# Delta rule, router and two expert layers on one core: the fourth key product in eight wide matmuls, the triangle solved by output rows, single first and last solve steps, and later key loads

## The chip, the cores and the metric

One Trainium2 chip; the program runs on one of its cores. The metric is device microseconds of one execution of the whole program.

## What is computed

Three layers follow one another: a delta rule over 4 x 8 heads of 768 tokens with 48 values each, a router with 8 experts of 384 x 1024, and a dense layer of 384 x 2048 with a squared relu. The change touches the first:

```
k_n = k / (norm(k) + 1e-6)
state = 0                                   # 48 x 48 for each of the 32 heads
for t in range(768):
    y[t]  = q[t] @ state
    v_old = state.T @ k_n[t]
    state = state + beta[t] * outer(k_n[t], v[t] - v_old)
x = y, as 3072 rows of 384
x = gate * (relu(x @ w1[expert]) @ w2[expert])    # expert = argmax of x_n @ e_n / tau
out = relu(x @ w_in) ** 2 @ w_out
```

## The kernel before, in words

The 768 tokens are cut into 24 chunks of 32, four chunks make a group (6 groups). Within a chunk the rule becomes a lower triangular system of 32 x 32 for each head, so that a group has 128 lanes (4 chunks x 32 heads and batches), one to a partition.

- **Products of keys** (`gram`, L138 to L185, called through `grams` at the start and in the chunk loop later): for each chunk 64 small TensorE matmuls of 64 x 32 against 32 columns (keys only, `n1 = 1`) or 64 columns (keys and queries). ScalarE evicts them (L169) into `GPs` (key by key, one tile per group) and `Pm` (key by query). For groups 0 and 1 VectorE turns `GPs` into lanes (L204, four 32 x 32 block transposes); for later groups that goes through DRAM (`gscr`, L171 and L174). `Pm` goes through DRAM for all groups (`pscr`, L179, then `PL2`, L183). These DMAs are on the queue of SP, which issues in order and waits for each one's input.
- **The solve** (`lanes`, L191 to L283): for one group a list of VectorE instructions. The norms come from the squares of the first keys (group 0) or from the diagonal of the products, by three Newton steps (`newton`, L78). `factors` (L223) makes `gam`; `scale` multiplies the products with its negative (L212). Then 31 steps in which `mul(j)` (L264) multiplies column j of the products with what is solved, and `acc(j)` (L272) adds it to the triangle `T`; four transposes (`end`, L277) put the result into `TTt`. Between the last steps stand `vh` (L254, values times norms) and `masked` (L189).
- **Order.** The instructions are issued in the order in which the Python calls are made. At the start (L728 to L783) the loads are issued, then `grams(0, 1, 0, 4, 0)`, 26 instructions of group 0's list, each followed by one of `route_q` (the router's own Newton steps on 8 rows), more products, and from the point at which 15 units of group 0's list are left, one instruction of group 1 before each of group 0.
- **The chunk loop** (L786 on): in each chunk VectorE makes `Ub` (L319) from `CH`, TensorE multiplies it with `TTt` (L338), ScalarE and VectorE evict that as `Wb` (L351, L319), TensorE updates the state (L357), ScalarE evicts it (`Sb`, L367), and the next chunk's `CH` is the state times its keys (L308). `fill` puts instructions of the groups ahead in between, by a budget that is worked out while the program is written.
- **Loads.** `load_kq` (L120) fetches keys and queries of a chunk, for chunks 0 to 14 on SP, from 15 on by GpSimd. Chunks 12 to 14 are fetched at L768, 15 to 17 at L856, in the code behind the first chunk, but nothing holds GpSimd until then. `padding` (L535) fills a piece of the router's table with one row by GpSimd; it is called in the chunk loop for chunks 0 to 8.
- **After the loop** the experts (each product in three fp32r matmuls of high and low parts) and the last layer run; TensorE is full there.

Of the kernel before, what the change touches and what calls it, by code (L numbers as in the profile page):

```python
# [8 lines left out]
F32 = mybir.dt.float32  # L9
# [13 lines left out]
def kernel(  # L23
# [54 lines left out]
    def newton(ops, y, ss, t, half):  # L78
        ops.append(lambda: V.tensor_scalar(y.bitcast(I32), ss.bitcast(I32), 1, None, ALU.logical_shift_right))
        ops.append(lambda: V.tensor_tensor(y.bitcast(I32), half, y.bitcast(I32), ALU.subtract))  # L80
        for _ in range(3):
            ops.append(lambda: V.tensor_tensor(t, y, ss, ALU.mult))
            ops.append(lambda: V.scalar_tensor_tensor(t, t, -0.5, y, ALU.mult, ALU.mult))
            ops.append(lambda: V.scalar_tensor_tensor(y, t, 1.5, y, ALU.add, ALU.mult))
        ops.append(lambda: V.tensor_tensor(y, y, ss, ALU.mult))
        ops.append(lambda: V.tensor_scalar(y, y, 1e-6, None, ALU.add))

# [53 lines left out]
    def gram(s, n0=0, n1=2, banks=GP2):  # L141
# [33 lines left out]
        if i == 3 and n1 == 2:  # L175
# [9 lines left out]
            )  # L185

    def masked(g, b):
        a = PL2[g][:, b].rearrange("p s c j -> p (s c) j")
        V.tensor_tensor(a, a, mask.unsqueeze(1).broadcast_to([128, 8, C]), ALU.mult)  # L189

    def lanes(g):  # L191
# [18 lines left out]
        def scaled(c0, c1):  # L210
            a = AL[:, c0:c1, c0 + 1 :]
            V.tensor_tensor(a, a, t1[:, c0 + 1 :].unsqueeze(1).broadcast_to(list(a.shape)), ALU.mult)  # L212

# [9 lines left out]
        def factors():  # L223
            add(lambda: V.reciprocal(r, nl))
            add(lambda: V.tensor_tensor(r, r, r, ALU.mult))
            add(lambda: V.tensor_tensor(gam, r, betaL[:, g], ALU.mult))
            add(lambda: V.tensor_scalar(t1, gam, -1.0, None, ALU.mult))

        nw = []
        if g == 0:  # L230
            add(lambda: V.tensor_reduce(ss, kn[0], AX.X, ALU.add))
            newton(nw, nn, ss, t1, magic)
# [28 lines left out]
        def mul(j):  # L261
            n, m = j + 1, 31 - j
            tv[0] = wp.tile([128, 256], F32, name=f"tmp{g % 2}")[:, : m * n].rearrange("p (c i) -> p c i", c=n)
            V.tensor_tensor(  # L264
                tv[0],
                AL[:, j, j + 1 :].unsqueeze(1).broadcast_to([128, n, m]),
                T[:, :n, j : j + 1].broadcast_to([128, n, m]),
                ALU.mult,
            )

        def acc(j):
            V.tensor_tensor(T[:, : j + 1, j + 1 :], T[:, : j + 1, j + 1 :], tv[0], ALU.add)  # L272

        def end(i):
            if i == 0:
                TTl[g] = wp.tile([128, C, C], F32, name="TTt", bufs=2)
            V.transpose(  # L277
                TTl[g].rearrange("p u i -> p i u")[:, i : i + 8], T.rearrange("p c i -> p i c")[:, i : i + 8]
            )

        for j in range(31):
            for f in (mul, acc):
                add(lambda f=f, j=j: f(j), (31 - j) * (j + 1))  # L283
# [367 lines left out]
    def attention():  # L651
# [91 lines left out]
        route_q.extend(router_consts())  # L743
        A.activation(kn[0], kn[0], AF.Square)
        consts()
# [11 lines left out]

        grams(0, 1, 0, 4, 0)
        st0 = Stream(0, 0)
        streams.append(st0)  # L760
        for _ in range(26):
            st0.pop()
            if len(route_q) > 1:
                route_q.popleft()()
        warm(2)
        grams(0, 2, 4, 8, 0)
        load_k2(0)
        grams(1, 2, 0, 4, 1)  # L768
        for s in range(12, 15):
            load_kq(s)  # L770
        load_v(1)
        load_k2(1)
        grams(0, 2, 8, 12, 1)
        st1 = Stream(1, 0)
# [12 lines left out]
        for s in range(NS):  # L787
# [61 lines left out]
            if last and i == 0:  # L849
                R[1]()  # L850
                queue(R[2])
                scats += R[3]
            if s <= E:
                padding(s)
            if s == 0:
                for n in range(15, 18):  # L856
                    load_kq(n)
            if i == 3 and g + 2 < NG:
# [597 lines left out]
```

## Time and profile before

| | |
|---|---|
| median of 3 runs | 931.98 us (930.43 to 934.85) |
| the profiled execution | 926.72 us |
| its span, from the first to the last instruction | 925.0 us |
| TensorE busy | 868.9 us (94%) |
| VectorE busy | 592.3 us (64%) |
| ScalarE busy | 443.2 us (48%) |
| GpSimd busy | 104.0 us (11%) |
| mean granted TensorE clock | 0.966 |

The shares are means over parts with different limits, so they are read by stretches. A line of the trace has the start and the duration in microseconds, the engine, the line of the program, the operation with the tile it writes, an arrow and the tiles it reads, the shape, and how many instructions it stands for; in brackets stands how long the engine was idle before it, and what ended that. PE is TensorE's matmul, PEld its weight load, DVE VectorE, ACT ScalarE, POOL GpSimd, SPq and POOLq the queues that issue DMAs.

### The profile page before, as it was taken

To read this page: it belongs to the slowest core of one execution; us is meant where nothing else is said; L and a number is where in the kernel's file an instruction comes from. 1 tells how busy PE (TensorE), PEld (TensorE's weight loads), DVE (VectorE), ACT (ScalarE), POOL (GpSimd) and SP (SyncE) were. 2 spreads that over 40 slices of the span, in tenths; PEclk is the share of its full clock that TensorE was granted. 3 is DMA by queue.
4 is the path that set the end of the run, shared out by engine and by line. 5 is a ranking of instruction groups with operands and counts; after the bars stand their busy time and mean duration, and the time that the engine had idled before them with its cause. 6 is when DMAs were issued, how large, how long until landed. Compare 5 with 4: busy or idle time off the path is not lost.

```text
span 925.0 us, 22005 instructions
## 1 busy us (share of the span) xinstructions
PE 868.9 (94%) x8859; PEld 792.9 (86%) x8859; DVE 592.3 (64%) x1478; ACT 443.2 (48%) x1074; POOL 104.0 (11%) x138
## 2 busy tenths in 40 slices
PE   3668999999989899999999999999999999999998
PEld 2446677667678799899988999999999999999998
DVE  6999799999767788879776762517061524425150
ACT  2246778778834565465645642415051423324140
POOL 3012103212211122122222100000000000000000
PEclk7587899999999999999999999999999999999999
DMA  8786876332247778557673532010010101020000
GB/s 328 247 270 204 237 196 189 117 142 70 75 147 183 266 267 285 181 198 274 223 243 102 175 83 43 1 45 7 28 25 18 35 18 35 9 43 10 18 1 26
DMA packets 103678, 117.12 MB, mean 127 GB/s; under 512 B 60339, under 2 KB 82202, under 8 KB 103568
## 3 DMA queue, kind: packets, MB, share of 16 engines
q1 hardware_dynamic: 95344, 89.25, 31.5%
q0 software_dynamic: 8064, 26.35, 7.9%
q8 instruction: 75, 1.23, 0.6%
q14 instruction: 35, 0.29, 0.1%
q10 hardware_dynamic: 160, 0.01, 0.0%
HBM read 83.47 MB, written 32.89 MB: 126 GB/s over the span
## 4 chain that ended last, share of the span: by engine, by line
PE 65%; DMA 1%; ACT 0%; another core or an unknown queue 0%; DVE 0%; SPq 0%; issue 0%; ACTq 0%
PE gp L1158 8%; PE gp L1159 8%; PE gp L1160 8%; PE xp L1158 5%; PE xp L1160 5%; PE xp L1159 5%; PE sp L1159 4%; PE sp L1158 4%; PE sp L1160 4%; PE yp L1159 3%; PE yp L1160 3%; PE yp L1158 3%; PE gp L1284 1%; PE ch L981 1%; PE ch L1158 1%; PE ch L1159 1%
## 5 line engine op out<-in xcount | busy, mean ns | idle before, releaser
L1364 DVE TENSOR_TENSOR t4k<-t2k 128x384 f32<-128x384 f32 x128 | 71.3, 557 | 203.8 <-ACT t2k L1363 201.9
L1158 PE MATMUL xp<-wb,hh 128*128 128x384 f32 x184 | 62.5, 340 | 0.0
L1159 PE MATMUL xp<-wb,hh 128*128 128x384 f32 x184 | 62.1, 338 | 0.0
L1160 PE MATMUL xp<-wb,hl 128*128 128x384 f32 x184 | 62.1, 338 | 0.0
L272 DVE TENSOR_TENSOR TL<-TL,tmp 128x135 f32<-128x135 f32 (+15 forms) x186 | 60.8, 337 | 1.8
L264 DVE TENSOR_TENSOR tmp<-AL,TL 128x135 f32<-128x135 f32 (+15 forms) x186 | 60.5, 336 | 1.6
L1307 POOL DMA_INDIRECT x<-y,rows x32 | 37.8, 1182 | 195.6 <-ACT y L1304 123.0
L1158 PE MATMUL sp<-xh,W 128*128 128x384 f32 (+1 forms) x156 | 53.1, 340 | 0.8 <-ACT xh L982 0.8
L1159 PE MATMUL sp<-xl,W 128*128 128x384 f32 (+1 forms) x156 | 53.0, 340 | 0.6 <-DVE xl L983 0.6
L1160 PE MATMUL sp<-xh,W 128*128 128x384 f32 (+1 forms) x156 | 53.0, 339 | 0.0
L1158 PE MATMUL gp<-wb,hh 128*128 128x384 f32 x152 | 51.7, 340 | 0.0
L1159 PE MATMUL gp<-wb,hh 128*128 128x384 f32 x152 | 51.3, 338 | 0.0
L1160 PE MATMUL gp<-wb,hl 128*128 128x384 f32 x152 | 51.3, 337 | 0.0
L367 ACT ACTIVATE Sb<-sp 48x384 f32<-48x384 f32 x92 | 44.7, 485 | 11.3 <-PE sp L357 9.9
L1160 PE MATMUL yp<-xh,W 128*128 128x384 f32 (+1 forms) x147 | 49.8, 339 | 0.0
L1159 PE MATMUL yp<-xl,W 128*128 128x384 f32 (+1 forms) x147 | 49.8, 339 | 0.0
L1158 PE MATMUL yp<-xh,W 128*128 128x384 f32 (+1 forms) x147 | 49.8, 339 | 0.0
L1388 ACT ACTIVATE y<-gp 128x384 f32<-128x384 f32 x12 | 5.9, 492 | 84.0 <-PE gp L1160 84.0
L1160 PE MATMUL gp<-xh,W 128*128 128x384 f32 (+1 forms) x135 | 45.7, 339 | 0.0
L1158 PE MATMUL gp<-xh,W 128*128 128x384 f32 (+1 forms) x135 | 45.7, 338 | 0.0
L1159 PE MATMUL gp<-xl,W 128*128 128x384 f32 (+1 forms) x135 | 45.7, 338 | 0.0
L1388 ACT ACTIVATE y<-xp 128x384 f32<-128x384 f32 x12 | 5.9, 492 | 81.6 <-PE xp L1160 81.6
(356 smaller groups left out, 2483.6 us busy)
## 6 DMA issues: line engine op xcount, KB each, us to landing
hb<-in_moe_w_dram SPq DMA_DIRECT2D x24, 384.0 KB
W<-wscr SPq DMA_DIRECT2D x16, 384.0 KB
W<-in_kq_dram SPq DMA_DIRECT2D x11, 512.0 KB
wscr<-t2k POOLq DMA_DIRECT2D x22, 256.0 KB, 5.6
xs<-padrow POOLq DMA_DIRECT2D x8, 693.0 KB, 8.5
W<-in_moe_w_dram SPq DMA_DIRECT2D x14, 384.0 KB
t4k<-in_moe_w_in_dram SPq DMA_DIRECT2D x10, 512.0 KB
W<-in_kq_dram POOLq DMA_DIRECT2D x9, 512.0 KB, 9.6
```

Source lines behind the costliest of these rows:

```text
L264: V.tensor_tensor(tv[0], AL[:, j, j + 1 :].unsqueeze(1).broadcast_to([128, n, m]), T[:, :n, j : j + 1].broadcast_to([128, n, m]), ALU.mult,)
L272: V.tensor_tensor(T[:, : j + 1, j + 1 :], T[:, : j + 1, j + 1 :], tv[0], ALU.add)
L367: A.activation(Sb[hq][r : r + D, :, :, par, :], SP_[hq][r : r + D, 0:384].rearrange("p (b m e) -> p b m e", b=4, m=2), AF.Copy,)
L981: PE.transpose(PT[kc][:, t * 128 : t * 128 + n], a[:, kc * 128 : (kc + 1) * 128], ident[:n, :n])
L1158: PE.matmul(ps, hs, rh, start=first, stop=False)
L1159: PE.matmul(ps, hs, rl, start=False, stop=False)
L1160: PE.matmul(ps, ls, rh, start=False, stop=last)
L1284: PE.matmul(ps[64 * r : 64 * r + 64, :DM], ht[:, 4 * r + fb], w2raw[e][4 * r + fb], start=fb == 0, stop=fb == 3,)
L1307: to_x2 = lambda n=n, t=t, y=y, e=e: G.indirect_dma_start(out=x2, out_offset=bass.IndirectOffsetOnAxis(ap=rows_i[:n, t, e : e + 1].bitcast ...
L1364: V.tensor_tensor(s2, r, r, ALU.mult)
L1388: A.activation(y, ps[:, :DM], AF.Copy)
```

## The change

- **Fourth key product.** Chunk 3's keys are multiplied by a new function: eight matmuls of 128 x 128 (all four batches against all four, of which the diagonal blocks are used) instead of 64, and eight evictions of 32 partitions instead of two of 128.
- **Order of the start.** The router's 12 Newton steps and three more come first on VectorE; the square of the first keys and its sum are made in two halves; one Newton step and the negation of `gam` are dropped (the scaling takes the factor -1 itself).
- **The triangle** is kept by output rows: `T[:, i, c]` instead of `T[:, c, i]`, so that the closing transposes read whole rows. The first solve step is one instruction (`gam` times a column), the last one also.
- **Loads.** Two paddings and chunks 15 to 17 are issued by GpSimd once it has copied an element that the eviction of chunk 7 wrote. On SP chunk 12 is fetched where chunks 12 to 14 were; 13, 14, and group 1's values and keys follow behind the products of chunks 8 to 11 and their DMAs. `padding` runs two chunks earlier.

```diff
+        for last in (False, False, True):
+            ops.append(lambda: nc.vector.tensor_tensor(t, y, ss, ALU.mult))
...
-        ops.append(lambda: V.tensor_tensor(y, y, ss, ALU.mult))
...
+    def gram_all(s, banks):
+        g, i = divmod(s, 4)
+        for p in range(4):
+            for h2 in range(2):
+                k = KQ[s][0][64 * h2 : 64 * h2 + 64, p].rearrange("d b j -> d (b j)")
+                PE.matmul(banks[h2][:, 128 * p : 128 * p + 128], k, k, start=True, stop=True)
+        for h2 in range(2):
+            for b in range(4):
+                rows = slice(C * b, C * b + C)
+                A.activation(
+                    GPs[g][rows, i].rearrange("p (x a c) j -> p c x a j", x=2, c=2)[:, h2],
+                    banks[h2][rows].rearrange("p (x a b j) -> p b x a j", x=2, a=2, b=4)[:, b],
+                    AF.Copy,
+                )
...
-            V.tensor_tensor(a, a, t1[:, c0 + 1 :].unsqueeze(1).broadcast_to(list(a.shape)), ALU.mult)
+            m = gam[:, c0 + 1 :].unsqueeze(1).broadcast_to(list(a.shape))
+            V.scalar_tensor_tensor(a, a, -1.0, m, ALU.mult, ALU.mult)
...
-            add(lambda: V.tensor_scalar(t1, gam, -1.0, None, ALU.mult))
...
-            add(lambda: V.tensor_reduce(ss, kn[0], AX.X, ALU.add))
+            for p in range(0, C, 16):
+                add(lambda p=p: V.tensor_reduce(ss[:, p : p + 16], kn[0][:, p : p + 16], AX.X, ALU.add))
...
-                AL[:, j, j + 1 :].unsqueeze(1).broadcast_to([128, n, m]),
-                T[:, :n, j : j + 1].broadcast_to([128, n, m]),
+                AL[:, j, j + 1 :].unsqueeze(2).broadcast_to([128, m, n]),
+                T[:, j : j + 1, :n].broadcast_to([128, m, n]),
...
-            V.tensor_tensor(T[:, : j + 1, j + 1 :], T[:, : j + 1, j + 1 :], tv[0], ALU.add)
+            V.tensor_tensor(T[:, j + 1 :, : j + 1], T[:, j + 1 :, : j + 1], tv[0], ALU.add)
...
-                TTl[g].rearrange("p u i -> p i u")[:, i : i + 8], T.rearrange("p c i -> p i c")[:, i : i + 8]
+                TTl[g].rearrange("p u i -> p i u")[:, i : i + 8], T[:, i : i + 8]
...
+        def both(j):
+            if j:
+                V.scalar_tensor_tensor(T[:, 31, :31], T[:, 30, :31], AL[:, 30, 31:], T[:, 31, :31], ALU.mult, ALU.add)
+            else:
+                V.tensor_scalar(T[:, 1:, 0], AL[:, 0, 1:], gam[:, 0:1], None, ALU.mult)
...
-            for f in (mul, acc):
+            for f in (mul, acc) if 0 < j < 30 else (both,):
...
-        grams(0, 1, 0, 4, 0)
+        grams(0, 1, 0, 3, 0)
+        gram_all(3, pairs[0])
+        turn_ += 1
+        while len(route_q) > 1:
+            route_q.popleft()()
...
         grams(0, 2, 4, 8, 0)
+        G.tensor_copy(pad[0:1, 0:1], Pm[1][0:1, 0, 3, 0, 0:1])
+        G.memset(pad[0:1, 0:1], 0.0)
+        for e in range(2):
+            padding(e)
         load_k2(0)
         grams(1, 2, 0, 4, 1)
-        for s in range(12, 15):
+        load_kq(12)
+        grams(0, 2, 8, 12, 1)
+        for s in range(13, 15):
             load_kq(s)
         load_v(1)
         load_k2(1)
-        grams(0, 2, 8, 12, 1)
+        for n in range(15, 18):
+            load_kq(n)
...
-            if s <= E:
-                padding(s)
-            if s == 0:
-                for n in range(15, 18):
-                    load_kq(n)
+            if s <= E - 2:
+                padding(s + 2)
```

VectorE at the start, before: the sum over the first keys (`sm<-vV`), then the router's steps (`es`) and group 0's (`sm`) in turn, and the first solve step in two instructions (rows between the Newton steps are left out).

```order
L231 TENSOR_REDUCE sm<-vV 128x32
L79 TENSOR_SCALAR es<-es 8x1
L79 TENSOR_SCALAR sm<-sm 128x32
L80 TENSOR_TENSOR es<-magic,es 8x1
L80 TENSOR_TENSOR sm<-magic,sm 128x32
...
L227 TENSOR_SCALAR sm<-sm 128x32
L238 COPY TL<-sm 128x32
L204 STREAM_TRANSPOSE AL<-GPs 128x256 x4
...
L264 TENSOR_TENSOR tmp_853<-AL,TL 128x31
L272 TENSOR_TENSOR TL<-TL,tmp_853 128x31
```

The same place with the change: all of the router's steps first, then the sum in two halves.

```order
L79 TENSOR_SCALAR es<-es 8x1
L80 TENSOR_TENSOR es<-magic,es 8x1
...
L578 TENSOR_SCALAR emb<-emb,es 8x384
L247 TENSOR_REDUCE sm<-vV 128x16 x2
L79 TENSOR_SCALAR sm<-sm 128x32
...
L242 TENSOR_TENSOR sm<-sm,betaL 128x32
L254 COPY TL<-sm 128x32
L219 STREAM_TRANSPOSE AL<-GPs 128x256 x4
...
L302 TENSOR_SCALAR TL<-AL,sm 128x31
```

The negation has gone, and the first solve step is the one instruction of L302.

VectorE between the `Ub` of chunks 19 and 20, the end of the last group's solve (`lg` and `rsm` are the router's; its rows are left out). Before, three solve steps in six instructions stand behind chunk 19's `Ub`:

```order
L319 TENSOR_TENSOR Ub_110<-ch_102,blk 128x768
L189 TENSOR_TENSOR PL_2745<-PL_2745,mask 128x256
L264 TENSOR_TENSOR tmp_4058<-AL,TL 128x87
L272 TENSOR_TENSOR TL<-TL,tmp_4058 128x29x3
L264 TENSOR_TENSOR tmp_4061<-AL,TL 128x60
L272 TENSOR_TENSOR TL<-TL,tmp_4061 128x30x2
L254 TENSOR_TENSOR vV<-vV,sm 128x384
L319 TENSOR_TENSOR Wb_113<-ch_103,blk 128x768
L189 TENSOR_TENSOR PL_2745<-PL_2745,mask 128x256
L264 TENSOR_TENSOR tmp_4103<-AL,TL 128x31
L272 TENSOR_TENSOR TL<-TL,tmp_4103 128x31
L277 STREAM_TRANSPOSE TTt<-TL 128x8x32 x2
```

With the change, the rows from the same `Ub` to the transposes:

```order
L342 TENSOR_TENSOR Ub_110<-ch_102,blk 128x768
L288 TENSOR_TENSOR TL<-TL,tmp_3982 128x3x29
L280 TENSOR_TENSOR tmp_4012<-AL,TL 128x60
L288 TENSOR_TENSOR TL<-TL,tmp_4012 128x2x30
L270 TENSOR_TENSOR vV<-vV,sm 128x384
L342 TENSOR_TENSOR Wb_113<-ch_103,blk 128x768
L204 TENSOR_TENSOR PL_2715<-PL_2715,mask 128x256
L300 SCALAR_TENSOR_TENSOR TL<-TL,AL 128x31
L293 STREAM_TRANSPOSE TTt<-TL 128x8x32 x3
```

Three instructions fewer lie between this `Ub` and the transposes.

The queue of SP, from the fetch of chunk 12 on, before:

```order
L126 DMA W<-in_kq_dram 128x1024 x3
L135 DMA vV<-in_v_dram 128x1536
L139 DMA kL_685<-in_k_dram 128x1536
L171 DMA gscr_66<-GPs 128x1024
L174 DMA AL<-gscr_66 32x32x32 x4
L179 DMA pscr_64<-Pm 32x4x256 x4
L183 DMA PL_842<-pscr_64 128x1024
```

and with the change:

```order
L125 DMA W<-in_kq_dram 128x1024
L170 DMA gscr_66<-GPs 128x1024
L173 DMA AL<-gscr_66 32x32x32 x4
L178 DMA pscr_64<-Pm 32x4x256 x4
L182 DMA PL_823<-pscr_64 128x1024
L125 DMA W<-in_kq_dram 128x1024 x2
L134 DMA vV<-in_v_dram 128x1536
L138 DMA kL_834<-in_k_dram 128x1536
```

The two later chunks, the values and the keys now stand behind group 2's way through DRAM.

## Rows read from the trace of the kernel before

**Rows 1.** Stretches: busy us (count) of PE, PEld, DVE, ACT, POOL; PEclk, DMA share, GB/s.

```profile
0.00:17.60 17.60, 6.87 (x267) 4.10 (x267) 9.28 (x51) 4.92 (x12) 7.93 (x30) 0.86 0.83 302
17.60:52.00 34.40, 21.00 (x793) 13.67 (x791) 33.30 (x120) 9.32 (x45) 0.00 (x0) 0.58 0.81 292
52.00:250.70 198.70, 179.65 (x4040) 136.31 (x4044) 184.85 (x629) 146.72 (x412) 40.22 (x50) 0.94 0.52 162
...
270.00:925.00 655.00, 645.35 (x3627) 625.74 (x3625) 349.88 (x627) 274.70 (x586) 51.10 (x55) 1.00 0.33 104
```

**Rows 2.** Timeline of the start: ACT's last step for the router, and VectorE.

```profile
7.09 0.18 ACT L550 ACTIVATION_READ_ACCUMULATOR junk<-emb 8x1 f32 x1
...
8.69 1.75 DVE L231 TENSOR_REDUCE sm<-vV 128x32 f32<-128x1536 f32 x1 [3.83 <-ACT vV L744]
...
10.36 0.13 DVE L79 TENSOR_SCALAR es<-es 8x1 int32<-8x1 int32 x1
...
13.38 0.21 DVE L235 STREAM_TRANSPOSE sm<-sm 128x32 f32<-128x32 f32 x1
...
14.66 0.19 DVE L238 COPY TL<-sm 128x32 f32<-128x32 f32 x1
...
17.63 2.08 DVE L204 STREAM_TRANSPOSE AL<-GPs 128x256 f32<-128x256 f32 x4 [2.78 <-ACT GPs L169]
```

**Rows 3.** Timeline of the start: TensorE's products of chunk 3.

```profile
9.90 0.32 PE L149 MATMUL gp<-W 64*32 64x32 f32 x21
...
16.54 0.71 PE L149 MATMUL gp<-W 64*32 64x32 f32 x43 [6.32 <-issue]
```

**Rows 4.** Timeline, VectorE at 285 us: Newton steps that depend on each other.

```profile
285.59 0.19 DVE L82 TENSOR_TENSOR t2k<-t2k 128x32 f32<-128x32 f32 x1
285.82 0.19 DVE L83 SCALAR_TENSOR_TENSOR t2k<-t2k 128x32 f32<-128x32 f32 x1
```

**Rows 5.** VectorE's instructions by form up to 265 us: busy us, mean ns, idle before.

```profile
L277 DVE STREAM_TRANSPOSE TTt<-TL 128x256 f32<-128x256 f32 x24 | 15.9, 684 | 0.0
...
L204 DVE STREAM_TRANSPOSE AL<-GPs 128x256 f32<-128x256 f32 x8 | 4.5, 594 | 3.0 <-ACT GPs L169 3.0
...
L264 DVE TENSOR_TENSOR tmp<-AL,TL 128x207 f32<-128x207 f32 x12 | 4.5, 374 | 0.1
L272 DVE TENSOR_TENSOR TL<-TL,tmp 128x207 f32<-128x207 f32 x12 | 4.4, 366 | 0.1
```

**Rows 6.** Timeline: three 128-column TensorE transposes, and four evictions of 32 partitions.

```profile
97.46 0.55 PE L412 MATMUL xp<-ident,XG 128*128 128x128 f32 x3
...
118.49 1.36 ACT L351 ACTIVATE Wb<-ch 32x192 f32<-32x192 f32 x4
```

**Rows 7.** VectorE's waits from 50 to 290 us (total us, times, longest).

```profile
DVE Ub L319 <- PE ch L308: 7.3, 6, 3.0
```

**Rows 8.** Timeline of the loop: the product L308 and the Ub behind it.

```profile
96.00 0.87 PE L308 MATMUL ch<-Sb,W 128*32 128x96 f32 x32
...
96.68 0.96 DVE L319 TENSOR_TENSOR Ub<-ch,blk 128x768 f32<-128x768 f32 x1 [2.97 <-PE ch L308]
...
212.57 0.87 PE L308 MATMUL ch<-Sb,W 128*32 128x96 f32 x32
...
213.88 0.96 DVE L319 TENSOR_TENSOR Ub<-ch,blk 128x768 f32<-128x768 f32 x1
```

**Rows 9.** Busy time in one stretch; columns as in rows 1, PEclk the granted clock.

```profile
87.90:94.60 6.70, 6.03 (x110) 5.23 (x114) 5.36 (x14) 3.01 (x12) 0.00 (x0) 0.50 0.61 194
```

**Rows 10.** Timeline: issues on SP's queue for group 2.

```profile
47.57 0.33 SPq L171 DMA_DIRECT2D gscr<-GPs  x1
...
68.04 0.34 SPq L183 DMA_DIRECT2D PL<-pscr  x1
```

**Rows 11.** Timeline: TensorE's W products of the second chunk.

```profile
66.13 0.86 PE L338 MATMUL ch<-Ub,TTt 128*32 128x192 f32 x16 [2.45 <-DVE Ub L319]
```

**Rows 12.** The page's list of DMA issues: KB each, median us from issue to landing.

```profile
W<-in_kq_dram POOLq DMA_DIRECT2D x9, 512.0 KB, 9.6
```

More of the change, by code (lines that the diff above doesn't have):

```diff
@@ L80, in newton @@
         ops.append(lambda: V.tensor_tensor(y.bitcast(I32), half, y.bitcast(I32), ALU.subtract))
[L81 to L84, printed above, removed]
-        ops.append(lambda: V.tensor_tensor(y, y, ss, ALU.mult))
-        ops.append(lambda: V.tensor_scalar(y, y, 1e-6, None, ALU.add))
+        for last in (False, False, True):
+            ops.append(lambda: nc.vector.tensor_tensor(t, y, ss, ALU.mult))
+            ops.append(lambda last=last: nc.vector.scalar_tensor_tensor(y if last else t, t, -0.5, y, ALU.mult, ALU.mult))
+            ops.append(lambda last=last: nc.vector.scalar_tensor_tensor(y, y if last else t, 1.5, t if last else y, ALU.add, ALU.mult))
+        ops.append(lambda: nc.vector.tensor_scalar(y, y, 1e-6, None, ALU.add))
     actx = ExitStack()
@@ L262, in mul @@
             n, m = j + 1, 31 - j
-            tv[0] = wp.tile([128, 256], F32, name=f"tmp{g % 2}")[:, : m * n].rearrange("p (c i) -> p c i", c=n)
+            tv[0] = wp.tile([128, 256], F32, name=f"tmp{g % 2}")[:, : m * n].rearrange("p (i c) -> p i c", c=n)
             V.tensor_tensor(
                 tv[0],
-                AL[:, j, j + 1 :].unsqueeze(1).broadcast_to([128, n, m]),
-                T[:, :n, j : j + 1].broadcast_to([128, n, m]),
+                AL[:, j, j + 1 :].unsqueeze(2).broadcast_to([128, m, n]),
+                T[:, j : j + 1, :n].broadcast_to([128, m, n]),
                 ALU.mult,
@@ L743, in attention @@
         route_q.extend(router_consts())
-        A.activation(kn[0], kn[0], AF.Square)
+        for p in range(2):
+            A.activation(kn[0][:, 16 * p : 16 * p + 16], kn[0][:, 16 * p : 16 * p + 16], AF.Square)
         consts()
@@ L756, in grams @@
                 warm(w)
-        grams(0, 1, 0, 4, 0)
+        grams(0, 1, 0, 3, 0)
[3 more added lines that the diff above has]
+            route_q.popleft()()
         st0 = Stream(0, 0)
         streams.append(st0)
-        for _ in range(26):
+        for _ in range(27):
             st0.pop()
-            if len(route_q) > 1:
-                route_q.popleft()()
         warm(2)
         grams(0, 2, 4, 8, 0)
+        G.tensor_copy(pad[0:1, 0:1], Pm[1][0:1, 0, 3, 0, 0:1])
+        G.memset(pad[0:1, 0:1], 0.0)
+        for e in range(2):
+            padding(e)
         load_k2(0)
         grams(1, 2, 0, 4, 1)
-        for s in range(12, 15):
+        load_kq(12)
+        grams(0, 2, 8, 12, 1)
+        for s in range(13, 15):
             load_kq(s)
```

## Prediction

> **What bounds the kernel.** I read the stretches first [rows 1]. From 270 us on TensorE is busy 645 of 655 us and VectorE 350, so that part moves as a block: what the change gains or loses before it, it keeps. From 52.0 to 250.7, the loop over 24 chunks, VectorE is busy 184.9 of 198.7 us, and from 17.6 to 52.0, where the first chunk's Ub starts, it is busy 33.3 of 34.4, while TensorE has 21.0. The delta rule is therefore VectorE's, and the change is priced on VectorE. The timeline of the start comes next [rows 2, 3]: VectorE has its factors ready at 14.66 and waits for products until 17.63; TensorE issued 21 of the 64 products of chunk 3 and then stood 6.32 us waiting for nothing that the profile shows. I take this for its supply of instructions: it stopped in the middle of a chunk whose data was there, and the DMA engines were 0.83 busy over the stretch. Then the form table for durations [rows 5] and the waits of the loop [rows 7, 8].
>
> **The start, up to the first transposes.** Removed: the 2.78 us wait. What now ends last there? (a) The products. 9 warm-ups (18 instructions), 192 products and 8 wide ones make 218 issued, fewer than the 18 + 192 + 21 that ran before the stop [rows 3], so the stop falls behind chunk 3. A wide one has 128 columns; the nearest row is a 128-column transpose, three in 0.55 us, so eight take 1.5 us, 3.0 if the clock halves [rows 6]. From 9.9 that ends at 11.4 to 12.9. Eight evictions of 32 partitions follow: 0.34 us each by the row of four in 1.36 (192 columns, so an upper bound), 0.17 if they run at half of that: 1.4 to 2.7 us. Ready at 12.8 to 15.6. (b) VectorE. The twelve 8-row steps now come first, from 7.3 (the accumulator read at 7.09 ends) [rows 2]. Such a step lasts 0.13 [rows 2], and a dependent one starts 0.04 after the end of its predecessor (0.23 between starts of 0.19 us steps [rows 4]): 12 x 0.17 = 2.0, plus an estimated 0.5 for two reciprocals and the scaling: 9.8. The two half reductions, together the 1.75 of the one plus 0.1, end at 11.6 (the halves of the square are done by then). Then twelve Newton steps instead of thirteen at 0.23, 2.8 us, and from the small transpose to the copy of the factors 1.1, since that was 13.38 to 14.66 [rows 2] with the negation and the scaling in between: 15.5. VectorE is the later one, and the transposes start at 15.5 instead of 17.63: **-2.1**. Bounds: 0, if products or the longer first chain end at 17.6; -2.8, if the factors are no later than before.
>
> **From the transposes to the first Ub (17.6 to 52.0)** VectorE is dense, with 0.2 us of waits, for products 4 to 7, that go (the stop of 6.32 falls early in chunk 4, where VectorE has ten microseconds of its own work ahead). Edits with one answer go together: the first solve step is one instruction instead of two, in groups 0 and 1, and so is the last one of group 0; group 1 loses a Newton step and the negation. An instruction that is removed is worth its 0.19 plus 0.04 where the next depends on it [rows 4], and about 0.08 less than 0.19 where the next is independent and starts early, as at 10.36, 0.08 before the reduction's end at 10.44 [rows 2]: 0.11 to 0.23. Five of them: -0.7. But one solve step of group 1 (207 elements, 0.37 and 0.37 [rows 5]) slides in front of the first Ub, since that stream is shorter: +0.66. Four closing transposes read whole rows now: 0.68 before; the other transpose, with one strided side, 0.59 [rows 5]. I take 0.59, because it is now the nearest shape: -0.36. Together with the wait: **-0.6**, Ub at 49.3. Bounds 0 (transposes unchanged, removed steps at 0.11) and -1.0.
>
> By the Trainium skill, "SBUF — State Buffer", section "Door 1: The DMA port swizzle", accesses that step past a 16-byte line pay a penalty, so that reading rows would be cheaper everywhere. The rows agree for the transposes alone: the product that reads a column of T lasts 0.374, the sum 0.366, at 207 elements [rows 5]. By the products' rows the transposes would gain nothing either, and the sum would be -4.0 instead of -5.7.
>
> **The loop.** I counted VectorE's instructions between consecutive Ub in both orders, priced each by its form's row less 0.08, and got -4.3 us over the 20 intervals that hold solve work. But an interval shrinks only as far as TensorE's side lets it: the gap between the time at which Ub could have started (0.68 after the first product of state and keys, as at 96.00 and 96.68) and its start. In interval 18 that is 213.88 - 213.25 = 0.63 [rows 8]. Six Ub waited for that product, 7.3 us in all [rows 7], four of them within these 20 intervals (2, 4, 6 and 19); the longest, 2.97 at 96.68 [rows 8], is interval 4. These four give nothing. Cut so, intervals 1 to 15 give -0.8 and 16 to 20, where the last group ends earlier (the order excerpt), -2.2: **-3.0**. Bounds: 0, and -4.3.
>
> **What costs nothing.** The gate's Newton step lies where VectorE has 300 us to spare [rows 1]. Scaling with a three-operand instruction: priced as before, the Newton rows of both kinds last 0.19 [rows 4]. Moved DMAs: the two paddings and three key loads leave the crowded start, and the loads of chunks 13 and 14 and of group 1's values and keys stand behind four waits on the SP queue; their cover is that chunk 13 is needed only behind the second chunk's W product, at 66.13 + 0.86 - 2.7 = 64.3 [rows 11]. Without it, see the third rival.
>
> Sum: -2.1 - 0.6 - 3.0 = **-5.7 us**, against the profiled execution of 926.72: 921.0. That execution is 5.3 below the median of the three runs, 931.98, so on the median's footing I forecast **926.3**.
>
> **Rivals.**
> 1. *The start gains little*: the wide products or their evictions are late, or the 8-row chain is slower than 0.17 a step. For: both bounds of (a) reach 15.6. Gain 3.6: 928.4.
> 2. *The loop is bound by TensorE's side.* For: the six waits [rows 7], and an interval 18 with 0.63 to spare [rows 8]. Gain 2.7: 929.3.
> 3. *The key loads come too late*, the case on the other side. Chunk 13's load now waits on SP for the round trips of group 2 through DRAM. Before, issuing those took from 47.57 to 68.04 [rows 10]. Begun 2.7 earlier and as slow, they end at 65.4; a key load lands 9.6 after its issue [rows 12], 75.0, 10.7 behind the 64.3 at which TensorE wants it, and interval 2 has no room. 926.3 + 10.7 = 937.0. It decides as soon as chunk 13 lands behind 64.3. Against: those 20.5 us began beside five loads (chunks 12 to 14, values and keys), of which four now stand behind the chain, and TensorE reaches chunk 11, with which it begins, without the stops that the crowded start cost it.
> 4. *The clock falls at other places.* At 87.9 to 94.6 the granted clock was 0.5 [rows 9], its lower level of 1.2 GHz, and interval 4 ended with the 2.97 us wait (its TensorE was busy 6.03 of 6.70 us). Fewer pauses may keep the clock up there: 923.3 if that wait goes [rows 8]. With the products done earlier, TensorE stands idle longer before the first Ub, and two more such waits may come: 931.3. The Trainium skill, "TensorE: Matmul & The Clock Gate", section "What's actually happening", says that an idle TensorE is clocked down; the rows agree, and do not say where it will happen.
>
> **How the numbers follow.** Chances: forecast 0.48 (own range 924 to 929), rival 1 0.12, rival 2 0.15, rival 3 0.07, rival 4 downwards 0.08 and upwards 0.10. The range, 920.5 to 931.5: with every term at its good end the gain is 8.1 (923.9), and about 921 with the 2.97 wait gone too; upwards it takes in rivals 1, 2 and 4 and leaves out rival 3. About 0.5% (4.7 us) is what a measurement of this kernel can tell from no change: faster than 927.3 are most of the forecast case, rival 4's good side and a little of 1 and 2, 0.55; slower than 936.6 is the bad end of rival 3, 0.05; between, 0.40.
>
> **What would show it.** Right: chunk 3's last eviction before 15.5, the transposes at about 15.5, the first Ub at about 49.3, the last Ub at about 245.0 instead of 250.7, and closing transposes at 0.59. Wrong in the first step if the transposes wait for ACT; in the loop if VectorE's waits for the product before Ub grow by what was removed; wrong altogether if TensorE waits for a key load in the second chunk, or if the part behind 270 us changes its length.

## The result, and the profile after

The changed kernel is slower: 934.26 us median (931.63 to 943.88, 11 runs) beside 932.2 of the kernel before in the same series (11 runs); the measured ratio of the two kernels is 1.0061, 95% interval 1.0035 to 1.0088. It isn't the quotient of these two medians, which is 1.0022: the slowdown is small, and its size is known only roughly. The median is outside the forecast range, on the other side. The profiled execution of the changed kernel, its median, has a span of 932.5 us; that of the kernel before has 925.0 and is a fast one, 5.3 us under the median of its first three runs. The stretches, columns as in [rows 1]:

```profile
0.00:17.60 17.60, 10.20 (x347) 6.36 (x347) 12.53 (x53) 7.50 (x23) 4.36 (x23) 0.92 0.83 312
17.60:52.00 34.40, 18.09 (x666) 11.65 (x663) 33.41 (x119) 7.61 (x36) 8.06 (x14) 0.55 0.85 295
52.00:250.70 198.70, 173.32 (x3871) 131.93 (x3869) 174.39 (x583) 140.71 (x399) 30.93 (x44) 0.91 0.50 159
...
270.00:925.00 655.00, 650.50 (x3651) 630.93 (x3650) 356.36 (x646) 275.70 (x588) 51.25 (x57) 1.00 0.33 104
```

In the same 198.7 us of the loop VectorE was busy 10.5 us less than before: it stood idle that much longer. The timeline of the start shows that the loss isn't there:

```profile
9.79 1.16 PE L192 MATMUL gp<-W 64*128 64x128 f32 x16
...
10.95 2.24 ACT L196 ACTIVATE GPs<-gp 32x128 f32<-32x128 f32 x8 [0.79 <-PE gp L192]
...
15.55 0.20 DVE L254 COPY TL<-sm 128x32 f32<-128x32 f32 x1
15.64 2.15 DVE L219 STREAM_TRANSPOSE AL<-GPs 128x256 f32<-128x256 f32 x4
```

The eight wide products (16 records in the trace) and their evictions are done at 13.2, VectorE's factors at 15.6, and the transposes start at 15.64 instead of 17.63 [rows 2]. What follows is read from the 24 starts of Ub, whose line is L342 now (timeline, VectorE; seven of them):

```profile
49.78 0.96 DVE L342 TENSOR_TENSOR Ub<-ch,blk 128x768 f32<-128x768 f32 x1
...
64.04 0.95 DVE L342 TENSOR_TENSOR Ub<-ch,blk 128x768 f32<-128x768 f32 x1
...
77.28 0.96 DVE L342 TENSOR_TENSOR Ub<-ch,blk 128x768 f32<-128x768 f32 x1 [0.71 <-PE ch L331]
...
129.04 0.96 DVE L342 TENSOR_TENSOR Ub<-ch,blk 128x768 f32<-128x768 f32 x1
...
139.10 0.96 DVE L342 TENSOR_TENSOR Ub<-ch,blk 128x768 f32<-128x768 f32 x1 [2.09 <-PE ch L331]
...
188.82 0.95 DVE L342 TENSOR_TENSOR Ub<-ch,blk 128x768 f32<-128x768 f32 x1
...
214.73 0.96 DVE L342 TENSOR_TENSOR Ub<-ch,blk 128x768 f32<-128x768 f32 x1 [1.15 <-PE ch L331]
```

The same in the kernel before, with the first copy of group 4's solve (L244), to which step 7 comes back:

```profile
52.04 0.98 DVE L319 TENSOR_TENSOR Ub<-ch,blk 128x768 f32<-128x768 f32 x1
...
75.30 0.96 DVE L319 TENSOR_TENSOR Ub<-ch,blk 128x768 f32<-128x768 f32 x1 [0.82 <-PE ch L308]
...
125.05 0.96 DVE L319 TENSOR_TENSOR Ub<-ch,blk 128x768 f32<-128x768 f32 x1
...
128.66 0.40 DVE L244 COPY sm<-AL 128x32 f32<-128x32 f32 x1
...
132.98 0.96 DVE L319 TENSOR_TENSOR Ub<-ch,blk 128x768 f32<-128x768 f32 x1
...
183.06 0.95 DVE L319 TENSOR_TENSOR Ub<-ch,blk 128x768 f32<-128x768 f32 x1
...
206.46 0.95 DVE L319 TENSOR_TENSOR Ub<-ch,blk 128x768 f32<-128x768 f32 x1
```

In the table and below, a step starts with its Ub, and what it takes is counted from the Ub of the step before.

| Ub of step | before | after | after minus before |
|---|---|---|---|
| 0 | 52.04 | 49.78 | -2.26 |
| 1 | 65.12 | 64.04 | -1.08 |
| 2 | 75.30 | 77.28 | +1.98 |
| 6 | 116.29 | 116.73 | +0.44 |
| 7 | 125.05 | 129.04 | +3.99 |
| 8 | 132.98 | 139.10 | +6.12 |
| 14 | 183.06 | 188.82 | +5.76 |
| 17 | 206.46 | 214.73 | +8.27 |
| 23 | 250.70 | 259.72 | +9.02 |

Behind the last Ub the changed kernel is 1.5 us shorter (672.8 against 674.3). So the loop lost 11.3 us, in three places: step 2 (3.1), steps 7 and 8 (5.7), steps 15 to 17 (2.5); the rest cancels. This is between two single executions: if the 0.61% of the ratio (5.7 us) are taken in place of their 7.5, with the same start and end, the loop's loss is about 9.5, an estimate. VectorE's waits from 17 to 270 us (total, times, longest; before: [rows 7]) name the first two, and TensorE's timeline shows the other half of step 2:

```profile
DVE Ub L342 <- PE ch L331: 9.2, 10, 2.1
DVE sm L260 <- DMA AL<-gscr: 4.3, 1, 4.3
DVE vV L270 <- DMA vV<-in_v_dram: 3.3, 1, 3.3
```

```profile
65.05 1.51 PE L361 MATMUL ch<-Ub,TTt 128*32 128x192 f32 x16 [4.83 <-DVE Ub L342]
68.85 1.18 PE L148 MATMUL gp<-W 64*32 64x64 f32 x64 [2.29 <-DMA W<-in_kq_dram]
```

*Step 2.* Chunk 13's keys and group 1's values (`vV`) come late. SP issued them at 64.33 and 65.34, behind the round trip of group 2 (`gscr` out, `AL` back, `pscr`, `PL`):

```profile
49.55 0.32 SPq L170 DMA_DIRECT2D gscr<-GPs  x1
54.34 5.53 SPq L173 DMA_DIRECT2D AL<-gscr  x4
59.97 1.99 SPq L178 DMA_DIRECT2D pscr<-Pm  x4
63.95 0.34 SPq L182 DMA_DIRECT2D PL<-pscr  x1
64.33 0.91 SPq L125 DMA_DIRECT2D W<-in_kq_dram  x2
65.34 0.38 SPq L134 DMA_DIRECT2D vV<-in_v_dram  x1
```

*Step 7.* On VectorE, the first copy of group 4's solve stands earlier in the order, ahead of step 7's Ub, and waits for its DMA, with Ub behind it:

```profile
128.35 0.19 DVE L260 COPY sm<-AL 128x32 f32<-128x32 f32 x1 [4.28 <-DMA AL<-gscr]
```

In the kernel before the same copy stands behind Ub and Wb of step 7, at 128.66, and waits for nothing. TensorE stood too, 2.29 us for the keys and 3.12 us for the Ub of step 7. The kernel before ran at half clock (0.50, the lower of the two levels) for 6.8 us of step 2 (67.4 to 74.2). Here the first such stretch is twice as long, and it began while TensorE waited 4.83 us for the Ub of step 1, ahead of the late loads; the second lies behind the wait in step 7:

```profile
62.40:76.04 13.64, 8.70 (x136) 6.51 (x137) 10.22 (x38) 4.90 (x15) 0.00 (x0) 0.50 0.63 251
130.70:137.50 6.80, 6.80 (x126) 5.38 (x118) 6.31 (x27) 4.46 (x14) 0.96 (x4) 0.50 0.67 226
```

*Steps 15 to 17.* VectorE has no wait above 1.2 us. From 201 us on it has only the last group's solve left, and each instruction starts when the one before has ended (0.43 us from start to start at 0.39 each):

```profile
201.32 0.39 DVE L288 TENSOR_TENSOR TL<-TL,tmp 128x220 f32<-128x220 f32 x1
201.75 0.40 DVE L280 TENSOR_TENSOR tmp<-AL,TL 128x231 f32<-128x231 f32 x1
202.18 0.40 DVE L288 TENSOR_TENSOR TL<-TL,tmp 128x231 f32<-128x231 f32 x1
```

### The profile page after: what moved, and what is told of

Read it like the earlier page. It is cut to its first block, busy times and chain, and to the rows that moved or that the text cites. A ratio compares the mean times of both kernels' runs of the same rounds, so it can differ in the third digit from the quotient of the medians.

```text
span 932.5 us, 21903 instructions
## 1 busy us (share of the span) xinstructions
PE 871.9 (93%) x8811; PEld 796.4 (85%) x8811; DVE 592.0 (63%) x1453; ACT 444.9 (48%) x1081; POOL 98.4 (11%) x140
## 4 chain that ended last, share of the span: by engine, by line
PE 66%; DMA 0%; issue 0%; ACT 0%; DVE 0%; ACTq 0%
PE gp L1188 8%; PE gp L1189 8%; PE gp L1190 8%; PE xp L1188 6%; PE xp L1189 6%; PE xp L1190 5%; PE sp L1189 4%; PE sp L1190 4%; PE sp L1188 4%; PE yp L1189 3%; PE yp L1188 3%; PE yp L1190 3%; PE gp L1314 1%; PE ch L1188 1%; PE ch L1189 1%; PE ch L1190 1%
## 5 line engine op out<-in xcount | busy, mean ns | idle before, releaser
L288 DVE TENSOR_TENSOR TL<-TL,tmp 128x135 f32<-128x135 f32 (+14 forms) x174 | 59.4, 348 | 1.8
L280 DVE TENSOR_TENSOR tmp<-AL,TL 128x135 f32<-128x135 f32 (+14 forms) x174 | 58.8, 345 | 1.8
L380 PE MATMUL sp<-Wb,kL 128*48 128x96 f32 x736 | 46.0, 278 | 0.4
```

What stands on the lines that cost most here:

```text
L280: V.tensor_tensor(tv[0], AL[:, j, j + 1 :].unsqueeze(2).broadcast_to([128, m, n]), T[:, j : j + 1, :n].broadcast_to([128, m, n]), ALU.mult,)
L288: V.tensor_tensor(T[:, j + 1 :, : j + 1], T[:, j + 1 :, : j + 1], tv[0], ALU.add)
L380: PE.matmul(SP_[hq][64 * par : 64 * par + D, b * 96 : b * 96 + 96], kL2[g][:, i, b * 2 + hq], Wb[hq].rearrange("p b (m r) e -> p b r m e", ...
```

## The experiments

Each kernel was timed beside the kernel before. Nineteen in twenty single executions lie within 6 us of the median of their series, the furthest 12 us away, so the ratios decide; an interval that holds 1 tells nothing from no change. A profile is one such execution and shows mechanisms. "Held" means that group 4's solve begins later, "spread" that the last group's solve is given out over more steps; both are explained below.

| run | what it is | ratio to the kernel before | 95% interval |
|---|---|---|---|
| (the change) | | 1.0061 | 1.0035 to 1.0088 |
| keys_first | change, key loads ahead of the round trip | 1.0055 | 1.0028 to 1.0081 |
| swap_loads | change, loads exchanged between SP and GpSimd | 1.0051 | 1.0022 to 1.0080 |
| pads_back | change, paddings one per step | 1.0080 | 1.0051 to 1.0109 |
| pads_late | change, paddings behind 77 us | 1.0086 | 1.0060 to 1.0113 |
| hold4 | change, group 4 held | 1.0009 | 0.9987 to 1.0032 |
| keys_hold4 | keys_first and hold4 | 1.0031 | 1.0004 to 1.0058 |
| swap_hold4 | swap_loads and hold4 | 1.0018 | 0.9986 to 1.0049 |
| swap_hold4_even | swap_hold4, spread | 0.9989 | 0.9959 to 1.0019 |
| pads_hold_even | pads_late, held, spread | 1.0007 | 0.9979 to 1.0036 |
| swap_even_pads | pads_back, exchanged, held, spread | 0.9983 | 0.9955 to 1.0012 |
| noload_hold_even | change without its loads, held, spread | 1.0018 | 0.9989 to 1.0048 |
| solve_only | before, new solve | 1.0008 | 0.9982 to 1.0033 |
| solve_hold_even | before, new solve, held, spread | 0.9983 | 0.9957 to 1.0008 |
| solve_hold_even_pads | solve_hold_even, late paddings | 1.0013 | 0.9985 to 1.0041 |
| start_only | before, new start and loads | 1.0036 | 1.0005 to 1.0067 |
| start_noload | before, new start | 1.0046 | 1.0019 to 1.0073 |
| loads_only | before, new loads | 1.0067 | 1.0039 to 1.0095 |
| before_pads | before, late paddings | 1.0040 | 1.0010 to 1.0070 |

**VectorE's order.** `hold4` begins group 4's solve at step 7.25:

```diff
-            while streams and budget > 0 or route_q:
-                if streams and budget > 0:
+            while streams and budget > 0 and now >= streams[0].since or route_q:
+                if streams and budget > 0 and now >= streams[0].since:
...
-                streams.append(Stream(made, s + 1.6))
+                streams.append(Stream(made, s + (2.2 if made == 4 else 1.6)))
```

> The changed kernel, with group 4's solve not begun before quarter step 7.25, so that its first copy stands behind step 7's Ub and Wb as in the kernel before. Theory B (an earlier place in VectorE's order put the copy ahead of its DMA): the 4.28 us wait for AL goes or falls under 1 us, step 7 starts 3 to 4 us earlier (129.0 to about 125.5), the half clock that followed it at 130.7 goes with it, and the time falls by 4 to 6 us, to 1.000 to 1.002 of the kernel before. Rival: the deferred steps are missing later, and the same time is lost in steps 8 to 12; the time stays at 1.006.

The copy waits for nothing now (timeline of VectorE, this run):

```profile
127.79 0.96 DVE L342 TENSOR_TENSOR Ub<-ch,blk 128x768 f32<-128x768 f32 x1 [3.49 <-PE ch L331]
...
131.98 0.18 DVE L260 COPY sm<-AL 128x32 f32<-128x32 f32 x1
```

In the profiled execution the Ub of step 7 came only 1.3 us earlier, not 3 to 4: it waited 3.49 us for TensorE instead, which ran at half clock (0.50) from 119.7 to 126.5 and was busy all that time. So the stretch at half clock moved and did not go; the loss of 2.1 in step 8 is gone. The time fell by 0.5% (4.8 us), and the intervals of the two ratios just don't overlap. Theory B holds for the wait and for the time. VectorE's waits for the DMA that fills AL add up to 1.3 to 4.3 us in all six versions with the new solve that are not held, and to 0 to 1.1 in the others.

`swap_hold4_even` adds one number to `swap_hold4` (the exchange is below), so that the planner's fixed pace (6.6 us of solve work a step) ends earlier:

```diff
-            pace = max(need(now), 8.0 if now < 3 else 6.6 if now < 16 else 0)
+            pace = max(need(now), 8.0 if now < 3 else 6.6 if now < 14.5 else 0)
```

> The exchange of loads and the held group 4 together. If A2 and B add: 0.997 to 0.999 of the kernel before. By rival D no better than the held group 4 alone: 1.000 to 1.002.

> As the run before, and the planner's fixed pace of 6.6 ends at step 14.5 instead of 16, so that the last group's solve is spread over steps 15 to 20. Theory E (a solve that runs alone on VectorE is a dependent chain, 0.45 us from start to start where two alternating streams need 0.34, and steps 17 to 20 are TensorE's anyway): steps 15 and 16 together take 15 to 16 us instead of 17.6, steps 17 to 20 stay at 7.2 each, and step 20 starts 1.5 to 2.5 us earlier than in the run before: 0.995 to 0.997. Rival: steps 17 to 20 lengthen by what 15 and 16 lose, and the time stays.

Ub of steps 14 to 16 without and with the number (timelines of VectorE):

```profile
181.08 0.96 DVE L342 TENSOR_TENSOR Ub<-ch,blk 128x768 f32<-128x768 f32 x1 [0.41 <-PE ch L331]
...
198.69 0.95 DVE L342 TENSOR_TENSOR Ub<-ch,blk 128x768 f32<-128x768 f32 x1
```

```profile
183.34 0.95 DVE L342 TENSOR_TENSOR Ub<-ch,blk 128x768 f32<-128x768 f32 x1
...
198.02 0.96 DVE L342 TENSOR_TENSOR Ub<-ch,blk 128x768 f32<-128x768 f32 x1 [0.19 <-PE ch L331]
```

Steps 15 and 16 take 14.7 us instead of 17.6, and 14.7 to 14.9 in the other runs with this number; steps 17 to 20 take 28.8 instead of 28.4: 2.5 us remain. Step 20 started only 0.2 us earlier than in the run before, since in this execution step 14 started 2.3 later. The ratio, 0.9989, is above the 0.995 to 0.997 expected; it moved by 0.3%, which one pair of intervals doesn't separate. Theory E holds for the steps, and that it shortens the time isn't shown. `swap_hold4` itself was no better than `hold4`.

The solve alone (`lanes` and `newton` of the change in the kernel before), without and with the two repairs:

> The kernel before, with the changed solve alone (triangle by output rows, first and last step single, Newton without its last product, scaling with three operands); products, loads and paddings as before. By the prediction's steps for the loop it gains 3 to 3.6 us: 0.996. By theory B the same shorter streams let group 4 begin earlier here too, in front of its DMA: a wait of 1 us or more for AL ahead of step 7's Ub, and 0.999 to 1.004. By rival C the clock decides and the ratio is anywhere within 0.3% of 1.

> The kernel before with the changed solve, group 4 held to step 7.25 and the planner's fixed pace ended at step 14.5; start and loads as before. By theories B and E it should be the best of the part versions: 0.996 to 0.998; steps 15 and 16 take 15 to 16 us together instead of 17.8 as in the run with the solve alone. If the solve's shorter work goes nowhere: 1.000.

Alone it gains nothing (1.0008): steps 15 and 16 take 17.8 us there too, and AL is waited for 1.3 us. Repaired it is at 0.9983, with `swap_even_pads` the lowest of all runs, and its interval still holds 1.

**The loads.** `keys_first` puts the loads of chunks 13 and 14 and of group 1 back ahead of the products of chunks 8 to 11 on SP; `swap_loads` lets GpSimd load chunks 12 to 14 and group 1's values behind its gate, and SP chunks 15 to 17.

```diff
-        load_kq(12)
-        grams(0, 2, 8, 12, 1)
-        for s in range(13, 15):
+        for s in range(12, 15):
             load_kq(s)
         load_v(1)
         load_k2(1)
+        grams(0, 2, 8, 12, 1)
```

> The changed kernel, with the loads of chunks 13 and 14 and of group 1's values and keys issued on SP where the kernel before issues them, ahead of group 2's round trip; nothing else undone. Theory A (these loads came too late): VectorE's 3.28 us wait for group 1's values and TensorE's 2.29 us wait for chunk 13's keys go, step 2 starts about 3 us earlier (77.3 to about 74), and the time falls by about 3 us, from 1.006 of the kernel before to about 1.003. VectorE's 4.28 us wait for group 4's AL stays. Rival C (the clock decides): the two waits go, but TensorE then waits as long for VectorE, is clocked down just the same, and the time stays within 1 us of the changed kernel's.

> Both of these edits. If A and B hold and add, the time falls by 7 to 9 us from the changed kernel's, to 0.997 to 0.999 of the kernel before; the start's 2.3 us are then kept at least in part. Rival C (the clock decides where the time goes): 1.003 or more.

> The changed kernel with two sets of loads exchanged: POOL, behind its gate at 24 us, loads chunks 12 to 14 and group 1's values (needed at 66 to 69 us) and SP loads chunks 15 to 17 (needed from about 85) behind group 2's round trip. Theory A2 (the loads have room only if they neither stand behind the round trip nor are queued together with it): VectorE's wait for group 1's values and TensorE's for chunk 13 are gone, the round trip of group 2 lands by 56 as in the changed kernel, step 1 stays within 0.5 us of 64.0 and step 2 starts at about 74 instead of 77.3: 3 us less than the changed kernel, 1.003. Rival D (DMA time is conserved: what is loaded early delays something else, as in the run with the keys first): another wait of 2 us or more appears before 80 us, and step 2 stays above 76.5.

With the keys first, the wait for chunk 13 is gone, that for the values is 1.7 us, and another takes their place: the first write of group 2's round trip lands 15 us after its issue instead of 5, ScalarE waits 7.8 us for it with the state behind, and TensorE for the state (timelines of SP, ScalarE and TensorE):

```profile
49.33 0.44 SPq L170 DMA_DIRECT2D gscr<-GPs  x1
64.45 2.62 SPq L173 DMA_DIRECT2D AL<-gscr  x4
```

```profile
64.54 0.45 ACT L168 ACTIVATE GPs<-gp 128x128 f32<-128x128 f32 x2 [7.82 <-DMA gscr<-GPs]
```

```profile
66.22 1.87 PE L331 MATMUL ch<-Sb,W 128*32 128x96 f32 x32 [6.11 <-ACT Sb L390]
```

With the loads exchanged the wait for values shrank to 1.3 us and none for keys is left, but the first Ub came 1.3 us later than in the changed kernel (51.03), and that of step 2 at 76.6, not 74. In neither did the time move by more than 0.1%, and with group 4 held as well the two are at 1.0031 and 1.0018, where the sum of A and B gave 0.997 to 0.999. So theory A isn't borne out: the waits are real, but neither run takes them away without putting something in their place, and what they cost by themselves stays open.

**The start and the loads, each alone** (the parts of the change named in the table, put into the kernel before):

> The changed kernel with the solve and the Newton steps of the kernel before (triangle by columns, all steps double); wide products, loads and paddings as changed. The first transposes start at about 15.9 and the first Ub at about 50.5. Theory B: the longer streams put group 4's copy behind step 7 again, so there is no wait for AL. Theory A: the waits for group 1's values and chunk 13's keys are there, 2 to 3 us each. Sum: start -1.5, key loads +3: 1.001 to 1.003 of the kernel before. If the loads were harmless: 0.998.

> The kernel before with the changed start alone: the wide products of chunk 3, the router's chain ahead of the reduction, the square in halves; solve, loads and paddings as before. Theory F (the start's microseconds are kept until VectorE's next wait, and the moved loads lose them): first Ub at 50 to 51, step 2 at or before the kernel before's 75.3, and 0.997 to 0.999. Theory G (an earlier start is lost whatever the loads do, because TensorE stands idle longer in step 1 and is clocked down): 1.001 to 1.004.

> The kernel before with the moved loads and paddings alone (gate on POOL behind chunk 7, chunks 13 and 14 and group 1's values and keys on SP behind group 2's round trip); products and solve as before. Theory F: the waits for group 1's values and chunk 13 appear, less what the later first Ub covers (each 1 to 3 us), and 1.002 to 1.004. Theory G: the loads are harmless here, 0.999 to 1.001.

> The changed kernel with its loads and paddings as before, group 4 held and the pace ended at 14.5: all of the change but the loads, with the two repairs of the order. By F, B and E: the start's 2 us and the solve's add: 0.994 to 0.997. By G: no better than the solve with the repairs, 0.997 to 1.000.

The new start alone is 0.46% slower, the new loads alone 0.67%, and both together 0.36%: they need one another. The ratios of all four runs, `noload_hold_even` with 1.0018 among them, lie above what the theories gave. Without the moved loads the wide products are as early, but TensorE then waits 10.8 us for chunk 4's keys, and the first Ub is at 52.88 (timeline of TensorE):

```profile
22.30 1.49 PE L149 MATMUL ch<-W 64*32 64x64 f32 x64 [10.76 <-DMA W<-in_kq_dram]
```

The loads alone bring the first Ub to 50.46 without a wide product, since TensorE's stop in the start is 4.32 us instead of 6.32 [rows 3], and then cost 5.3 us on VectorE and 5.2 on TensorE in step 2 (timelines):

```profile
75.54 0.56 DVE L254 TENSOR_TENSOR vV<-vV,sm 128x384 f32<-128x384 f32 x1 [5.31 <-DMA vV<-in_v_dram]
```

```profile
72.44 1.18 PE L149 MATMUL gp<-W 64*32 64x64 f32 x64 [5.21 <-DMA W<-in_kq_dram]
```

So theories F and G are both half right, as far as single profiles show: the moved loads lose the start's microseconds, and the start without them has none to lose. With both (`start_only`) the first Ub is at 50.50 and that of step 2 at 77.16, beside 52.04 and 75.30: the start's gain is lost by step 2 without the new solve, and the kernel is slower than before.

**Bytes.** Until 76 us the changed kernel moves 21.4 MB, the kernel before 20.0 (282 and 263 GB/s over the stretch): two paddings more.

> The changed kernel with no padding before the key loads of chunks 18 to 20 (at about 77 us); the nine paddings stand behind those, in front of and behind the loads of chunks 21 to 23, and in step 7. Theory H (bytes bound the DMA until step 2): 3.5 MB less to move until 76 us, the waits for group 1's values (3.28 us) and chunk 13 (2.29 us) fall under 1 us each, step 2 starts at 73.5 to 75 instead of 77.3; 1.001 to 1.003. AL of group 4 is still waited for. Rival (order and clock, not bytes): the waits stay within 1 us of what they were, 1.005 to 1.007.

> The same with the two repairs of VectorE's order (group 4 held to 7.25, fixed pace ended at 14.5). By H, B and E together: 0.993 to 0.996. By the rival: 0.999 to 1.002.

> The kernel before with its paddings at the same late places, nothing else. By H: 2.1 MB less until 76 us, ACT's wait for group 2's round trip (4.1 us) and the 2.8 us wait of the first transposes shrink; 0.996 to 0.998. By the rival: 0.999 to 1.001.

> The changed solve with the two repairs and the late paddings; start and loads as in the kernel before. By H, B and E: 0.994 to 0.997, about the sum of this one's parts (0.9983 without the paddings). By the rival 0.998.

> The changed kernel with the paddings emitted one per step as in the kernel before (the gate and the key loads of chunks 15 to 17 behind it stay). By theory H two paddings, 1.4 MB, at the 0.37 to 0.41 MB per us at which the DMA engines run here are 3.4 to 3.8 us less until 76 us: the waits for group 1's values and chunk 13 fall by 2 us or more together, step 2 starts at 74 to 75.5, and 1.002 to 1.004, with AL of group 4 still waited for. By the rival (bytes do not matter, the loads stand in a queue behind a round trip): waits and time as in the changed kernel, 1.005 to 1.007.

> The changed kernel with the loads exchanged, group 4 held, the fixed pace ended at 14.5 and the paddings one per step. By H the start's 2 us now stay: 0.994 to 0.997. By the rival as without the paddings' change: 0.998 to 1.000.

With all paddings late, step 3 started 3.5 us earlier than in the changed kernel (82.4 against 85.9), but the paddings then filled 76 to 90 us (DMA share 0.99, 0.73 in the changed kernel), TensorE stopped for 4 us with nothing that the profile shows, and step 4 took 15.3 us instead of 11.8. The first row is that stretch (columns as in [rows 1]), the second TensorE's timeline:

```profile
76.00:90.00 14.00, 9.09 (x320) 7.22 (x321) 13.55 (x41) 8.56 (x28) 5.93 (x11) 0.95 0.99 332
```

```profile
90.82 0.46 PE L148 MATMUL gp<-W 64*32 64x64 f32 x13 [3.96 <-issue]
```

With the paddings one per step the bytes are those of before, yet the waits for values (4.2 us) and chunk 13 (2.3) stay: behind the round trip these loads are late with 1.4 MB less as well. With 3.6 MB less (`pads_late`) the wait for chunk 13 is gone and that for values is 1.6 us, so the bytes count too, but the time got no better (1.0086). The late paddings alone make the kernel before 0.4% slower (`before_pads`), which neither side expected, and the repaired solve no faster (`solve_hold_even_pads`, 1.0013). Theory H falls as an account of the time. With the paddings one per step and the loads exchanged, both waits are gone and step 3 is 2.6 us ahead of the kernel before, which step 4 takes back; 0.9983.

## Why the prediction was wrong

**The start, -2.1 and -0.6: right up to the first Ub.** Measured -1.99 (17.63 to 15.64) and -0.27, first Ub 2.26 us earlier; the second term is half of what was forecast and within its bounds. TensorE's stop did not come early in chunk 4, as the prediction had it: there TensorE waited 3.73 us for the keys, and the first stop, 3.50 us, came after two products of chunk 6. The wide products took 1.16 us (estimated 1.5), their evictions 2.24 (1.4 to 2.7), VectorE's chain ended where it was forecast. Closing transposes took 0.61 (0.59 forecast), products and sums by rows 0.36 and 0.37, as by columns [rows 5] (mean of a form, changed kernel):

```profile
L293 DVE STREAM_TRANSPOSE TTt<-TL 128x256 f32<-128x256 f32 x24 | 14.1, 610 | 0.0
...
L288 DVE TENSOR_TENSOR TL<-TL,tmp 128x207 f32<-128x207 f32 x12 | 4.4, 371 | 0.1
L280 DVE TENSOR_TENSOR tmp<-AL,TL 128x207 f32<-128x207 f32 x12 | 4.3, 362 | 0.0
```

**The loop, -3.0: the step that failed.** It measured +11.3 between the two profiled executions (+8.7 in intervals 1 to 15, +2.0 in 16 to 20, +0.6 behind them), and failed twice.

1. "Intervals 1 to 15 give -0.8" measured +8.7. It compared VectorE's work with TensorE's slack. Shorter streams also move what stands behind them forward, and no moved instruction was asked what it waits for. Group 4's copy went ahead of step 7's Ub and met its DMA: a wait of 4.28 us, with steps 7 and 8 5.7 us longer. Holding that group took 0.5% off the time; five pairs of runs with and without the repairs of the order (`hold4`, `keys_hold4`, `swap_hold4`, `pads_hold_even`, `swap_even_pads`) all fell, by 0.24% to 0.97% (the last pair also exchanges the loads), and in three of them the intervals don't overlap. Of the rest, 3.1 us are step 2, whose late loads the prediction had put at nothing.
2. "Intervals 16 to 20: -2.2" measured +2.0. The work saved was taken from steps 17 to 20, which TensorE paces (7.2 to 7.4 us each from 18 on, with Ub waiting for its product), and given to steps 15 and 16, which VectorE paces. And the price of a form less 0.08 holds only while two streams alternate; alone, a 220-element instruction costs 0.43 from start to start, not 0.31. Here independent instructions start up to 0.1 us before the end of the one ahead (10.36 in [rows 2] is one), and in the lone chain the next starts 0.04 behind it (201.75 above). The Trainium skill, "VectorE: DVE Perf Modes", section "The DRAIN you can't avoid", says that the next instruction does not start until the pipeline is empty, and that one that is not held starts earlier; the trace shows starts of both kinds.

**"What costs nothing": wrong.** The third rival had the mechanism: SP came to chunk 13's load at 64.3 (65.4 worked out), and the keys landed 4.5 us behind the 64.3 at which the prediction had TensorE want them, not 10.7; TensorE, late itself, waited 2.29 us. The argument against this rival held, since the round trip's issues took 14.4 us instead of 20.5. But the trip began at 49.55 and not at the 44.9 that was assumed, so that its end moved by 1.4 us only. Group 1's values stand in the same queue and were not priced at all: 3.28 us. That this rival's 937.0 is not far from what was measured is luck: step 2 is 3.1 of the 11.3 us. How much of the time hangs on these loads stays open: with the paddings, and added to the kernel before by themselves, they cost 0.67%, and the runs of the changed kernel that took the two waits away were no faster.

The fourth rival's bad side came too, behind the first Ub and not before it: TensorE stood idle 4.83 us in step 1, and its clock fell to half at 62.4. The Trainium skill, "TensorE: Matmul & The Clock Gate", section "What's actually happening", says of an idle TensorE that it is clocked down, and the trace agrees. How much of step 2 that cost was not separated. (Two more waits of 2.97 us would have made this rival 932.2, not 931.3.)

**The part behind the loop** was called a block that keeps what the change gains or loses; it was 1.5 us shorter, which lies within what single executions differ by.

**What stays open.** Why the start's 2.3 us never reach the end, even with repaired order (`swap_hold4_even` and `swap_even_pads` are no faster than the solve alone repaired): in the profiles they go before the first Ub (51.99 in `swap_hold4_even`), in step 2 or in step 4, by a late load, a stop of TensorE or its half clock, each time another. No version beat the kernel before by more than the measurement can tell; the best repaired ones have a ratio 0.8% under that of the change.

## What to carry to other kernels

Where a planner fills an in-order engine, shorter work moves everything behind it forward: look up, for each instruction that passes a critical one, which DMA it waits for. Saved work counts only in the steps that its engine paces, and a chain that is left alone is priced from start to start (0.43 us here), not by the spacing seen between interleaved chains (0.31). A load moved behind a round trip in one queue waits for the whole trip, 14.8 us here.

## What the runs showed of the hardware that was not expected

TensorE's stops with nothing that the rows name end with the arrival of instructions. The page of the changed kernel lists, among the DMA queues, one whose packets are instructions (packets, MB, share of 16 engines):

```profile
q8 instruction: 75, 1.23, 0.5%
```

In the DMA records of all 20 profiled executions, up to 300 us, each of the 137 such stops of 0.9 us or more ends 1.2 to 1.7 us after one of these packets has landed; of TensorE's 205 other waits of that length 12% do. The 6.32 us of [rows 3] are one: the packet ran from 14.17 to 15.18, and TensorE went on at 16.54. So what the prediction took the stop for, its supply of instructions, fits the trace. A packet takes 1.0 us in the crowded start as behind 300 us (medians); this one began only 4.0 us after TensorE had stopped.

That DMA traffic is what delays these packets isn't shown. With the early loads moved away (`loads_only`) the first stop was 4.32 us instead of 6.32, but the stops up to 52 us add up to 19.9 us, beside 14.2 in the kernel before. A stop of 3.96 us came where six paddings and the key loads filled the DMA engines (share 0.99).
